# Joining two pairs of attention blocks in a fused attention and gated feed-forward kernel, and moving batches 2 and 3 to other slots

## The chip, the cores and the metric

The kernel runs on one core of one Trainium2 chip, in one launch. The metric is the device time of that launch in microseconds, and the figure that counts is the median over several executions. A profiled execution of the same program is shown as well; its time is given beside the span that its trace covers.

## The reference

Two blocks follow each other. The first is a polysketch attention with 4 batches, 4 heads, 1088 positions and a head size of 32. The second is a feed-forward block with a sigmoid gate over the 4 x 1088 = 4352 tokens that the first one gives, with a model size of 128 and an inner size of 1536.

```python
def phi(x):                       # r = 8, so 64 features
    a = np.einsum('rd,bhsd->bhsr', S1, x)
    b = np.einsum('rd,bhsd->bhsr', S2, x)
    return np.einsum('bhsi,bhsj->bhsij', a, b).reshape(*x.shape[:-1], r * r)
q_p, k_p = phi(q), phi(k)
kv  = np.einsum('bhsf,bhsd->bhfd', k_p, v)
z   = np.sum(k_p, axis=2)
num = np.einsum('bhsf,bhfd->bhsd', q_p, kv)
den = np.einsum('bhsf,bhf->bhs', q_p, z)[..., None] + 1e-06
x   = (num / den).transpose(0, 2, 1, 3).reshape(B * S, H * D)
out = (1 / (1 + np.exp(-(x @ w_gate))) * (x @ w_val)) @ w_out
```

The weights and the two sketch matrices come in as 64-bit floats and are turned into 32-bit ones on the chip.

## The kernel before

**The feed-forward part is the stream.** The tokens are cut into chunks of 512 (the last one 256). For each chunk, a *wave* (`w1`, L525 to L603) computes 128 gate columns and 128 value columns for all its tokens: four matmuls `wave<-xT,w_sb`, each on 64 of the 128 columns of TensorE's array, so that two run side by side. ScalarE takes the sigmoid of the gate (`sg`, L548), and VectorE multiplies (`g`, L583). There are 12 waves to a chunk (6 for the last), 102 in all, and a wave is called here by its number from 0, and so is the *slot* that ends with it. `slot` (L610) issues for each wave: the multiplication of the wave before, up to one late step of the result's sums, the output products that have come due, and then the wave. The output products of two waves (`w2_a`, `w2_b`, L460 and L490) are seven matmuls of 64 columns of weights against 256 tokens, four in one slot and three in the next; seven take the place of eight, for which GpSimd forms differences of `g` (`tsum`, L367) and VectorE sums of the results (`res`, L479). The waves have two PSUM buffers in the pool `psm`, tag `wave`.

**The attention is fed into the stream** in blocks between the waves, one batch after the other. For batch b:

- `load_kq(b)` and `load_v(b)` bring k, q and v into SBUF on SP's queue, `turn_k` and `turn_q` (two pieces, 512 and 576 wide) transpose them on VectorE.
- `begin(b)` (L1232) computes, on TensorE, the sketches of k (`kps`, 8 matmuls of 64 rows x 32 columns) and of q (`qcomp`: `cqps`, 8 matmuls likewise). ScalarE copies the second to SBUF (`cq`), and from there it is written to DRAM (`dq`). `spread(b)` (L834) reads it back in repeated form into `qp` and `bq`, and into the small tiles `A8` and `B8`: 14 loads on SP's queue, each of which also waits until the eighth load before it has landed.
- `outer(b, 0)` and `outer(b, 1)` multiply k's sketches into features (`KP`), `sum_z` adds them up, `qmult(b, 0)` and `qmult(b, 1)` multiply `qp` by `bq`.
- `kv(b)` (L888) is 36 matmuls of 128 rows x 32 columns against 64 features and 4 more for z; `kvd` copies the result out on ScalarE; `ndt` (L939) turns it with two matmuls of 128 x 64; `weights_z` (L993) prepares z on VectorE.
- `parts(b)` (L1266) is the last group: `den_j` (8 matmuls of 64 x 32 and a product on VectorE, `pd`), the numerators (`nps` in a wave buffer, `nps2`), `den_i` (2 matmuls), a copy of the numerators on ScalarE (`num`), and on VectorE the division, `turn_den` and then the products into `xT`, which the waves read.

All of kps, kv, ndt, denj and nps2 share one PSUM buffer (pool `ps2`, tag `two`). The tile `kq` of pool `ld` holds in turn k and q of a batch and its `bq`. `num` shares the buffer of `KP`.

**The order is written by hand.** Each of TensorE, VectorE, ScalarE and GpSimd executes its instructions in the order of the program text; SP's queue is ordered by the framework. For batches 2 and 3 the loop at L1344 takes the slot of each step from the table `plan` (L1342): `until(n)` issues slots until wave n is next. For batch 2: turn_k 27, turn_q 29 and 30, begin 31, outer 32 and 34, sum_z 36 and 37, kv 38, ndt 39, qmult 39 and 42, parts 44; for batch 3: 48, 49 and 51, 53, 56 and 57, 58 and 59, 60, 61, 61 and 63, 68. Batch 1 has begin at 13, kv at 18, ndt at 19, parts at 22.

```python
slot(lambda: ndt(1), 1)
slot(None, 1)
qmult(1, 1)
load_kq(2)
slot(None, 1)
slot(lambda: parts(1), 1)
```

Of the kernel before, what the change touches and what calls it, by code (L numbers as in the profile page):

```python
# [16 lines left out]
P = 128  # L17
# [3 lines left out]
def kernel(  # L21
# [31 lines left out]
    ld = ctx.enter_context(tc.tile_pool(name="ld", bufs=1))  # L53
    sbA = ctx.enter_context(tc.tile_pool(name="sbA", bufs=2))
    raw = ctx.enter_context(tc.tile_pool(name="raw", bufs=NJ // 2))
    sbN = ctx.enter_context(tc.tile_pool(name="sbN", bufs=1))
    sbG = ctx.enter_context(tc.tile_pool(name="sbG", bufs=3))

    dram = ctx.enter_context(tc.tile_pool(name="dram", bufs=1, space=bass.MemoryType.DRAM))

# [203 lines left out]
    k_t, q_t = {}, {}  # L264


    def new_kq(b):
        t = ld.tile([P, 2 * H * W1], F32, tag="kq", name="kq")
        kq = t[:, : 2 * T * D].rearrange("p (a t d) -> p a t d", a=2, t=T)
        k_t[b], q_t[b] = kq[:, 0], kq[:, 1]  # L270

# [20 lines left out]
    def warm(*cols):  # L292
        t = psm.tile([P, 2, 512], F32, tag="wave", name="warm")
        x = nc.const_aps.tensor(1.0, [P, P], F32)
        for n in cols:
            r = nc.const_aps.tensor(1.0, [P, n], F32)
            nc.tensor.matmul(out=t[:, 0, :n], lhsT=x, rhs=r, start=True, stop=True)  # L297
# [362 lines left out]
    WD = 160  # L660
    mask = {}

    def kps(b):
        t = ps2.tile([P, 2, 512], F32, tag="two", name="kps")
        ts = [t[:, 0], t[:, 1]]
        turns = [(g, pi) for g in range(4) for pi in range(2)]

        if b == 0:
            ts[1] = pso.tile([P, TCH], F32, tag="acc1", name="kps1")
            turns.sort(key=lambda x: x[1])  # L670
        for g, pi in turns:
            rows = slice(64 * pi, 64 * pi + 64)
            nc.tensor.matmul(  # L673
                out=ts[pi][32 * g : 32 * g + 32, : NJK * 32],
                lhsT=sk[rows, :],
                rhs=kT_of[b][rows, KBASE[g] : KBASE[g] + NJK],
                start=True,
                stop=True,
            )

        KAB[b] = sbA.tile([P, 2, NJK, 32], F32, tag="kab", name="kab")
        for pi in range(2):
            nc.vector.transpose(
                out=KAB[b][:, pi].rearrange("p j c -> p (j c)"), in_=ts[pi][:, : NJK * 32]
            )
        KP[b] = sbA.tile([P, 2, NJK, 2, F], F32, tag="kp", name="kp", bufs=1)
# [147 lines left out]
    def spread(b, ns, cq, put, get):  # L834
        p0 = 64 * ns[0]
        d = dram.tile([P, 2, W1], F32, tag="dq", name="dq")
        put.dma_start(out=d[p0:], in_=cq[p0:])
        for n in ns:
            for i, t in enumerate((QP[b], BQ[b])):

                for c in (0, 1) if i else (0,):
                    d0 = d[64 * n + 32 * c + 2 * i, 0]
                    rows = [[0, R], [8 * W1, R]] if i else [[8 * W1, 2 * R], [0, R]]
                    get.dma_start(  # L844
                        out=t[64 * c : 64 * c + 64 if i else P, n * H * W1 : (n + 1) * H * W1],
                        in_=bass.AP(
                            tensor=d0.tensor, offset=d0.offset, ap=rows + [[1, H * W1]]
                        ),
                    )
        if len(ns) < 2:  # L850
            return
        put = get

        B8[b] = sbA.tile([P, W1], F32, tag="b8", name="b8", bufs=1)
        A8[b] = sbA.tile([P, 2, WD], F32, tag="a8", name="a8", bufs=1)
        for x in range(2):
            for m in range(2):
                p0 = 64 * x + 32 * m
                for i, t in enumerate((A8[b], B8[b])):
                    d0 = d[2 * i + m, 0]  # L860
                    if i == 0:
                        offset, run = d0.offset + (W1 - WD) * x, [[W1, 2], [1, WD]]
                    else:
                        offset, run = d0.offset + W1 * x, [[1, W1]]
                    put.dma_start(
                        out=t[p0 : p0 + 32],
                        in_=bass.AP(tensor=d0.tensor, offset=offset, ap=[[8 * W1, 32]] + run),
                    )
# [16 lines left out]
                    skip_group_check=True,  # L885
                )

    def kv(b, zsum):  # L888
        kvz = KVZ[b] = ps2.tile([P, 2, 512], F32, tag="two", name="kvz")[:, 0]
        for j in [1, 2, 3, 4, 5, 6, 7, 8, 0]:  # L890
            for h in range(H):
                nc.tensor.matmul(  # L892
                    out=kvz[32 * h : 32 * h + 32, :F],
                    lhsT=v_sb[:, h, j, :],
                    rhs=KP[b][:, h // 2, j, h % 2, :],
                    start=(j == 1),
                    stop=(j == 0),
                    skip_group_check=True,
                )
        for h in range(H):  # L900
            nc.tensor.matmul(
                out=kvz[32 * h : 32 * h + 32, F : 2 * F],
                lhsT=nc.const_aps.tensor(1.0, [P, 32], F32),
                rhs=zsum[:, h, :],
                start=False,
                stop=True,
                skip_group_check=True,
            )
# [242 lines left out]
        start=True,  # L1151
        stop=True,
    )
    warm(64)
    st_ = st_[:, : 2 * R].rearrange("p (n r) -> p n r", n=2)
    sk = const.tile([P, 2, 2, R], F32, tag="sk")
    nc.vector.tensor_tensor(
# [71 lines left out]
    slot(None, 1)  # L1229
    cq = {}  # L1230

    def begin(b):  # L1232
        glu()
        kps(b)
        cq[b] = qcomp(b, (0, 1), (psm, "wave"))
        spread(b, (0, 1), cq[b], nc.scalar, nc.sync)

# [25 lines left out]
                    stop=True,  # L1263
                )

    def parts(b):  # L1266
        den_j(b)
        glu()
        t = psm.tile([P, 2, 512], F32, tag="wave", name="nps")
        numerators(b, t, False)  # L1270
        num = sbA.tile([P, 2, NJK, 2, F], F32, tag="kp", name="num", bufs=1)
        num = num.rearrange("p c j m f -> p (c j m f)")[:, :1024].rearrange("p (c w) -> p c w", c=2)
        nc.scalar.copy(out=num, in_=t)
        t = ps2.tile([P, 2, 512], F32, tag="two", name="nps2")
        numerators(b, t[:, :, WD : WD + 32], True)
        turn_den(b, den_i(b, t[:, 0, :WD]))
        for n in range(2):
            rb = sbA.tile([P, 9, 2, 32], F32, tag="rb", name="rb")
            t0, tn = q_chk[n]
            r0 = RC[b][:, n]  # L1280
            nc.vector.transpose(
                out=rb[:, :tn].rearrange("p t c s -> p (t c s)"),
                in_=bass.AP(
                    tensor=r0.tensor,
                    offset=r0.offset,
                    ap=[list(r0.ap[0]), [1, 2 * tn], [0, 32]],
                ),
            )
            for u0, u1, x in ((0, 8, num[:, :, 256 * n : 256 * n + 256]), (8, tn, t[:, :, WD : WD + 32])):
                if u0 < u1:  # L1290
                    o = b * S + 64 * (t0 + u0)
                    nc.vector.tensor_tensor(
                        out=xT[:, o : o + 64 * (u1 - u0)].rearrange("p (t c s) -> p c t s", c=2, s=32),
                        in0=x.rearrange("p c (t s) -> p c t s", s=32),
                        in1=rb[:, u0:u1].rearrange("p t c s -> p c t s"),
                        op=MUL,
                    )
        moe["ready"] = b * S + S
# [10 lines left out]
    load_kq(1)  # L1309
    slot(None, 1)  # L1310
    slot(lambda: part01(lambda: narrow_w(NJ - 1, 3)), 1)
    slot(last01, 1)
    load_v(1)
    turn_k(1)
    slot(None, 1)
    turn_q(1, 0)
# [12 lines left out]
    qmult(1, 0)  # L1329
    weights_z(1)  # L1330
    slot(lambda: ndt(1), 1)
    slot(None, 1)
    qmult(1, 1)
    load_kq(2)
    slot(None, 1)
    slot(lambda: parts(1), 1)
    moe["store"]()
# [1 line left out]
    def until(n):  # L1339
        slot(None, n - moe["n"])  # L1340

    plan = {2: (27, 29, 30, 31, 32, 34, 36, 37, 38, 39, 42, 44)}  # L1342
    plan[3] = (48, 49, 51, 53, 56, 57, 58, 59, 60, 61, 63, 68)
    for b in range(2, B):  # L1344
        at = iter(plan[b])
        until(next(at))
        turn_k(b)
        for n in range(2):
            until(next(at))
            turn_q(b, n)  # L1350
        until(next(at))
        slot(lambda: begin(b), 1)
        for pi in range(2):
            until(next(at))
            outer(b, pi)
        for step in range(2):
            until(next(at))
            sum_z(b, step)
        until(next(at))
        slot(lambda: kv_all(b), 1)  # L1360
        if b + 1 < B:
            load_v(b + 1)
        until(next(at))
        qmult(b, 0)
        slot(lambda: ndt(b), 1)
        weights_z(b)
        until(next(at))
        qmult(b, 1)
        load_kq(b + 1)
        until(next(at))  # L1370
        slot(lambda: parts(b), 1)
    slot(None, 10**3)


# [28 lines left out]
```

## Time and profile before

| | |
|---|---|
| median of 3 executions | 292.4 us (292.35 to 292.85) |
| profiled execution, its own time | 296.02 us |
| span of its trace | 294.1 us |
| TensorE clock granted, mean | 0.999 |
| TensorE busy | 288.8 us, 98% of the span |
| VectorE busy | 186.5 us, 63% |
| GpSimd busy | 160.6 us, 55% |
| ScalarE busy | 93.7 us, 32% |
| DMA | 24.23 MB, 82 GB/s over the span |

The trace lists each instruction with its engine (PE for TensorE's matmuls, PEld for its weight loads, DVE for VectorE, ACT for ScalarE, POOL for GpSimd, SPq and ACTq for the loads that these two issue), the line of the code, the tiles that it writes and reads, its form and how many were merged into a row. Times are microseconds from the first instruction; a bracket says how long the engine stood idle before, and what ended that. A matmul in 32-bit floats makes two records. The ends of matmuls are modelled and include their way through the array, so the start of one to the start of the next tells more than the length of a record.

### The profile page before, as it was taken

What the parts mean: (1) busy time and instruction counts of PE and PEld (TensorE: products, weight loads), DVE (VectorE), ACT (ScalarE), POOL (GpSimd) and SP (SyncE); (2) the same over time, 40 slices, a digit from 0 to 9 for tenths busy, and PEclk for the clock granted to TensorE, in tenths of its full rate; (3) what the DMA queues carried; (4) which work ended last, traced back from release to release, by engine and by line L of the source; (5) the groups of instructions that cost most, each with busy time, mean ns of one, the idle gap of its engine ahead of it and who ended that gap; (6) DMA issues with size and microseconds to landing.
All of it is one profiled execution on the core that took longest, in us unless ns stands there. A gap on an engine that the chain in (4) does not pass through costs nothing.

```text
span 294.1 us, 5762 instructions
## 1 busy us (share of the span) xinstructions
PE 288.8 (98%) x2264; PEld 156.6 (53%) x2264; DVE 186.5 (63%) x316; ACT 93.7 (32%) x172; POOL 160.6 (55%) x222
## 2 busy tenths in 40 slices
PE   8989999999999999999999999999999999999995
PEld 3543433355455455545555555554555555555895
DVE  5778789885656766677556696667436423552482
ACT  3386542321324222323224222323223223322321
POOL 2266544796535657655456498555456565646300
PEclk9999999999999999999999999999999999999999
DMA  7993613295640168416000474202000200020003
GB/s 219 347 336 68 150 39 125 74 180 137 186 97 0 19 163 159 133 50 177 12 0 2 129 174 106 37 0 38 1 0 2 36 2 0 0 31 7 0 4 54
DMA packets 28890, 24.23 MB, mean 82 GB/s; under 512 B 18560, under 2 KB 24064, under 8 KB 28864
## 3 DMA queue, kind: packets, MB, share of 16 engines
q1 hardware_dynamic: 25808, 21.95, 30.1%
q10 hardware_dynamic: 3056, 1.92, 2.3%
q8 instruction: 18, 0.29, 0.4%
q14 instruction: 8, 0.07, 0.1%
HBM read 20.60 MB, written 3.26 MB: 81 GB/s over the span
## 4 chain that ended last, share of the span: by engine, by line
PE 89%; DMA 7%; SPq 1%; DVE 0%; issue 0%; ACT 0%; DVEq 0%
PE wave L540 55%; PE prod L377 20%; DMA bq<-dq 5%; PE moeout L421 4%; PE moeout L447 2%; PE warm L297 1%; PE kps L673 1%; SPq L844 1%; PE nps L1258 1%; DMA s_in<-in_S_dram 1%; PE kvz L892 1%; PE cqps L819 1%; DMA dq<-cq 1%; DMA b<-dq 1%; PE denj L1021 0%; PE dps L1063 0%
## 5 line engine op out<-in xcount | busy, mean ns | idle before, releaser
L540 PE MATMUL wave<-xT,w_sb 128*64 128x512 f32 (+3 forms) x820 | 210.6, 566 | 0.0
L540 PEld LDWEIGHTS wave<-xT,w_sb 128*64 128x64 f32 (+1 forms) x820 | 85.4, 140 | 63.2 <-issue 51.0
L548 ACT ACTIVATE sg<-wave 128x512 f32<-128x512 f32 x102 | 60.9, 597 | 171.1 <-PE wave L540 163.2
L583 DVE TENSOR_TENSOR g<-wave,sg 128x512 f32<-128x512 f32 x96 | 65.9, 686 | 76.3 <-ACT sg L548 75.0
L367 POOL TENSOR_TENSOR tsum<-g 128x256 f32<-128x256 f32 x84 | 67.9, 810 | 29.7 <-DVE g L583 29.6
L367 POOL TENSOR_TENSOR tsum<-g,tsum 128x256 f32<-128x256 f32 x42 | 34.2, 814 | 57.8 <-DVE g L583 57.6
L377 PE MATMUL prod<-tsum,ws 128*64 128x256 f32 x252 | 62.8, 381 | 0.0
L377 PEld LDWEIGHTS prod<-tsum,ws 128*64 128x64 f32 x252 | 31.2, 137 | 16.0 <-issue 11.8
L377 PE MATMUL prod<-g,w_sb 128*64 128x256 f32 x168 | 34.7, 381 | 0.0
L367 POOL TENSOR_TENSOR tsum<-tsum,g 128x256 f32<-128x256 f32 x42 | 32.7, 779 | 3.3
L377 PE MATMUL prod<-tsum,w_sb 128*64 128x256 f32 x84 | 25.3, 383 | 0.0
L377 PEld LDWEIGHTS prod<-g,w_sb 128*64 128x64 f32 x168 | 16.0, 136 | 17.5 <-issue 14.7
L377 PE MATMUL prod<-g,ws 128*64 128x256 f32 x84 | 25.0, 379 | 0.0
L117 POOL TENSOR_TENSOR head<-head,tail 128x384 int32<-128x384 int32 (+1 forms) x10 | 9.9, 987 | 13.9 <-DVE head L111 12.6
L377 PEld LDWEIGHTS prod<-g,ws 128*64 128x64 f32 x84 | 11.5, 137 | 3.7
L421 PE MATMUL moeout<-g,w_sb 128*128 128x512 f32 (+1 forms) x28 | 12.5, 603 | 0.0
L377 PEld LDWEIGHTS prod<-tsum,w_sb 128*64 128x64 f32 x84 | 10.8, 137 | 3.0 <-issue 2.2
L872 DVE TENSOR_TENSOR qp<-qp,bq 128x1152 f32<-128x1152 f32 (+1 forms) x7 | 9.4, 1344 | 4.6 <-DMA a<-dq 4.6
L752 DVE TENSOR_TENSOR kp<-kab 128x1152 f32<-128x1152 f32 (+2 forms) x10 | 10.9, 1101 | 0.0
L576 DVE TENSOR_TENSOR g<-wave,sg 128x512 f32<-128x512 f32 x6 | 6.7, 1121 | 4.6 <-ACT sg L548 4.6
L479 DVE TENSOR_TENSOR res<-prod,other 64x512 f32<-64x512 f32 (+1 forms) x14 | 7.6, 544 | 3.1 <-DMA a<-dq 1.6
L514 DVE STREAM_TRANSPOSE o_sb<-res 64x512 f32<-64x512 f32 x14 | 9.6, 688 | 0.0
(129 smaller groups left out, 209.6 us busy)
## 6 DMA issues: line engine op xcount, KB each, us to landing
qp<-dq SPq DMA_DIRECT2D x7, 576.0 KB
bq<-dq SPq DMA_DIRECT2D x14, 288.0 KB
kq<-in_k_dram SPq DMA_DIRECT2D x3, 544.0 KB
kq<-in_q_dram SPq DMA_DIRECT2D x3, 544.0 KB
w_in<-in_moe_w_out_dram SPq DMA_DIRECT2D x6, 256.0 KB
w_in<-in_moe_w_gate_dram SPq DMA_DIRECT2D x5, 256.0 KB
w_in<-in_moe_w_val_dram SPq DMA_DIRECT2D x5, 256.0 KB
v<-in_v_dram SPq DMA_DIRECT2D x8, 144.0 KB
```

The costliest lines, as they stand in the source:

```text
L117: nc.gpsimd.tensor_tensor(out=head, in0=head, in1=tail, op=ALU.add)
L367: nc.gpsimd.tensor_tensor(out=t[:, u], in0=in0, in1=in1, op=ALU.subtract)
L377: nc.tensor.matmul(out=out, lhsT=lhsT, rhs=rhs, start=start, stop=stop, skip_group_check=True)
L421: nc.tensor.matmul(out=moe["acc"][d], lhsT=w_sb[:, 2, j, d], rhs=g[:, jj], start=(j == 0), stop=(j == NJ - 1),)
L479: nc.vector.tensor_tensor(out=out, in0=in0, in1=in1, op=op)
L514: nc.vector.transpose(out=o_sb[:64, d].rearrange("p t x -> p (t x)"), in_=r[:, 1 + 2 * d : 3 + 2 * d].rearrange("p u x -> p (u x)"),)
L540: nc.tensor.matmul(out=wv[d, which, jj * tw + o : jj * tw + o + tp], lhsT=w_sb[:, which, j0 + jj, d], rhs=xT[:, t0 + o : t0 + o + tp], sta ...
L548: nc.scalar.activation(out=sg, in_=wv[:, 0], func=ACTF.Sigmoid)
L576: nc.vector.tensor_tensor(out=g.rearrange("p (j u s y) -> p j y u s", j=2, u=2, y=4), in0=wv[:, 1].rearrange("p (j y u s) -> p j y u s", j ...
L583: nc.vector.tensor_tensor(out=g, in0=wv[:, 1], in1=sg, op=MUL)
L752: eng.tensor_tensor(out=KP[b][:, pi, j0:j1].rearrange("p j m (i l) -> p (j m) i l", i=R), in0=bass.AP(tensor=a0.tensor, offset=a0.offset, ...
L872: nc.vector.tensor_tensor(out=q0, in0=q0, in1=half(BQ[b], n), op=MUL)
```

## The change

**Two joined places.** `kps` takes an argument `also`: the kv of another batch is then written into free columns of the same PSUM tile, ahead of kps's own matmuls. `begin(3, 2)` uses it, so that kv(2) and the projections of batch 3 are one block at slot 35. `parts` takes the same argument: `parts(2, 3)` at slot 45 puts kv(3) between the second numerators and `den_i`, in free columns of their tile, and the copy of `num` behind it.

**Other slots.** The loop and its table are gone; the steps are written one by one. Batch 2: turn_k 20, turn_q 21 and 23, begin 24, outer 25 and 26, sum_z 28 and 30, kv 35, weights_z 36, ndt 37, qmult 38 and 44, parts 45. Batch 3: turn_k 32, turn_q 33, begin 35, outer 36 and 37, sum_z 40 and 42, kv 45, ndt 48, qmult 50 and 52, parts 56. On VectorE turn_k(2) now stands between g(18) and g(19), turn_q(2, 0) between qmult(1, 1) and g(20), and turn_q(2, 1) between the division of parts(1) and g(22).

**Loads and memory.** `load_kq(2)` stands behind `load_v(1)`, ahead of spread(1) on SP's queue; `load_kq(3)` at slot 23. k and q of batches 2 and 3 get a tile of their own (`kq2`) in a new pool `late`, which takes the space that the conversion of the weights (`sbN`) used, and so do A8 and B8 of batch 3. bq(3) shares its tile with bq(2) and waits for qmult(2, 1).

**At the start** a matmul that only keeps TensorE busy, `warm`, has 128 columns in place of 64.

```diff
+    late_pool = []
+
     def new_kq(b):
-        t = ld.tile([P, 2 * H * W1], F32, tag="kq", name="kq")
+        pool, tag, w = (ld, "kq", 2 * H * W1) if b < 2 else (late_pool[0], "kq2", 2 * T * D)
+        t = pool.tile([P, w], F32, tag=tag, name="kq")
...
-    def kps(b):
+    def kps(b, also=None):
         t = ps2.tile([P, 2, 512], F32, tag="two", name="kps")
+        if also is not None:
+            kv(also, ZS[also], t[:, 0, NJK * 32 : NJK * 32 + 2 * F])
...
-        B8[b] = sbA.tile([P, W1], F32, tag="b8", name="b8", bufs=1)
-        A8[b] = sbA.tile([P, 2, WD], F32, tag="a8", name="a8", bufs=1)
+        pool = late_pool[0] if b == B - 1 else sbA
+        B8[b] = pool.tile([P, W1], F32, tag="b8", name="b8", bufs=1)
+        A8[b] = pool.tile([P, 2, WD], F32, tag="a8", name="a8", bufs=1)
...
-    warm(64)
+    warm(128)
...
-    def begin(b):
+    def begin(b, also=None):
         glu()
-        kps(b)
+        kps(b, also)
+        if also is not None:
+            kvd(also)
...
-    def parts(b):
+    def parts(b, also=None):
...
-        nc.scalar.copy(out=num, in_=t)
+        first = t
         t = ps2.tile([P, 2, 512], F32, tag="two", name="nps2")
         numerators(b, t[:, :, WD : WD + 32], True)
+        if also is not None:
+            kv(also, ZS[also], t[:, 1, 4 * F : 6 * F])
+        nc.scalar.copy(out=num, in_=first)
         turn_den(b, den_i(b, t[:, 0, :WD]))
+        if also is not None:
+            kvd(also)
...
     slot(lambda: part01(lambda: narrow_w(NJ - 1, 3)), 1)
+    top.close()
+    late_pool.append(ctx.enter_context(tc.tile_pool(name="late", bufs=1)))
     slot(last01, 1)
     load_v(1)
+    load_kq(2)
     turn_k(1)
...
     slot(lambda: ndt(1), 1)
+    turn_k(2)
     slot(None, 1)
     qmult(1, 1)
-    load_kq(2)
+    turn_q(2, 0)
     slot(None, 1)
     slot(lambda: parts(1), 1)
...
+    until(23)
+    turn_q(2, 1)
+    load_kq(3)
+    until(24)
+    slot(lambda: begin(2), 1)
+    features(2, 25, 26, 28, 30)
+    until(32)
+    turn_k(3)
+    until(33)
+    turn_q(3, 0)
+    turn_q(3, 1)
+    until(35)
+    slot(lambda: begin(3, 2), 1)
+    load_v(3)
+    until(36)
+    weights_z(2)
+    outer(3, 0)
+    until(37)
+    outer(3, 1)
+    slot(lambda: ndt(2), 1)
+    qmult(2, 0)
+    until(40)
+    sum_z(3, 0)
+    until(42)
+    sum_z(3, 1)
+    until(44)
+    qmult(2, 1)
+    until(45)
+    slot(lambda: parts(2, 3), 1)
+    until(48)
+    weights_z(3)
+    slot(lambda: ndt(3), 1)
+    until(50)
+    qmult(3, 0)
+    until(52)
+    qmult(3, 1)
+    until(56)
+    slot(lambda: parts(3), 1)
```

More of the change, by code (lines that the diff above doesn't have):

```diff
@@ L55 @@
     raw = ctx.enter_context(tc.tile_pool(name="raw", bufs=NJ // 2))
-    sbN = ctx.enter_context(tc.tile_pool(name="sbN", bufs=1))
     sbG = ctx.enter_context(tc.tile_pool(name="sbG", bufs=3))
+    top = ExitStack()
+    sbN = top.enter_context(tc.tile_pool(name="sbN", bufs=1))
     dram = ctx.enter_context(tc.tile_pool(name="dram", bufs=1, space=bass.MemoryType.DRAM))
@@ L886, in kv0, with kv @@
                 )
-    def kv(b, zsum):
-        kvz = KVZ[b] = ps2.tile([P, 2, 512], F32, tag="two", name="kvz")[:, 0]
+    def kv(b, zsum, kvz=None):
+        if kvz is None:
+            kvz = ps2.tile([P, 2, 512], F32, tag="two", name="kvz")[:, 0]
+        KVZ[b] = kvz
         for j in [1, 2, 3, 4, 5, 6, 7, 8, 0]:
@@ L1340, in until, with features @@
         slot(None, n - moe["n"])
[L1342 to L1371, printed above, removed]
+    def features(b, *at):
+        steps = [(outer, 0), (outer, 1), (sum_z, 0), (sum_z, 1)]
+        for n, (step, i) in zip(at, steps):
+            until(n)
+            step(b, i)
+    until(23)
[36 more added lines that the diff above has]
+    slot(lambda: parts(3), 1)
     slot(None, 10**3)
```

## The prediction

> **What bounds the kernel now.** I read the page first: engine shares, then the chain that ended last.
>
> ```profile
> PE 288.8 (98%) x2264; PEld 156.6 (53%) x2264; DVE 186.5 (63%) x316; ACT 93.7 (32%) x172; POOL 160.6 (55%) x222
> ...
> PE 89%; DMA 7%; SPq 1%; DVE 0%; issue 0%; ACT 0%; DVEq 0%
> ```
>
> TensorE is the bound; the other engines matter only where they make it wait. So three things can move the time: TensorE's own work, what it loses at each change of tile shape, and its few waits. In the chain in order of time, an undisturbed stretch gives the price of work:
>
> ```profile
> 230.92 1.72 PE wave L540 x8
> ...
> 240.81 1.72 PE wave L540 x8
> ```
>
> Four waves with their products take 240.81 - 230.92 = 9.89 us, 2.47 a slot. A wave is 8 records of 512 columns on two column halves side by side in 1.72 us: 0.43 us for a record of 512 columns. By that price a kv block (40 matmuls of two records, 64 columns, four at a time) needs 20 x 64 columns, 1.07 us; kps and cqps 0.48 each; a parts block (denj 0.27, nps 0.86, nps2 0.05, den_i 0.27) 1.45. The timeline of TensorE around kv(2) shows what it really costs:
>
> ```profile
> 118.05 1.94 PE L540 MATMUL wave<-xT,w_sb 128*64 128x512 f32 x8
> 119.92 1.21 PE L892 MATMUL kvz<-kp,v 128*32 128x64 f32 x72
> 120.95 0.29 PE L901 MATMUL kvz<-zs,const-float32-1.0 128*32 128x64 f32 x8
> 121.17 0.65 PE L377 MATMUL prod<-g,w_sb 128*64 128x256 f32 x4
> ```
>
> The wave's last column enters at 118.05 + 1.72 = 119.77, the products resume at 121.17: 1.40 us for 1.07 of work, 0.33 lost on the way in and out. In the same way begin(2) (101.30 to 102.52) loses 0.25 and parts(2) (136.53 to 138.38) 0.40. ndt, which keeps the stream's shape, takes its own 0.22 and loses nothing.
>
> The one large wait is at parts(1). TensorE's timeline there, then VectorE's:
>
> ```profile
> 75.89 0.48 PE L1021 MATMUL denj<-b,zw 64*32 64x160 f32 x8
> 76.79 0.48 PE L1021 MATMUL denj<-b,zw 64*32 64x160 f32 x8 [0.42 <-DMA b<-dq]
> 77.06 1.16 PE L1258 MATMUL nps<-qp,nd 64*32 64x512 f32 x32
> 78.15 0.49 PE L1034 MATMUL nps<-pd,head 128*64 128x160 f32 x4
> ```
>
> ```profile
> 75.05 1.36 DVE L872 TENSOR_TENSOR qp<-qp,bq 128x1152 f32<-128x1152 f32 x1 [2.62 <-DMA a<-dq]
> 76.32 0.68 DVE L583 TENSOR_TENSOR g<-wave,sg 128x512 f32<-128x512 f32 x1
> 77.32 0.49 DVE L1029 TENSOR_TENSOR pd<-denj,a 128x320 f32<-128x320 f32 x1 [0.31 <-PE denj L1021]
> 77.73 0.68 DVE L583 TENSOR_TENSOR g<-wave,sg 128x512 f32<-128x512 f32 x1
> ```
>
> TensorE is there at 75.86 and resumes the products at 78.47: 2.6 us for 1.45 of work, about 0.8 more than parts(2) loses. Two things end this wait together. The last b8 piece lets denj finish (76.79 + 0.27 = 77.06). And nps takes the wave buffer of slot 20, which g(20) frees at 76.32 + 0.68 = 77.00; g(20) stands behind qmult(1,1), which stood for its data until 75.05.
>
> [...] 0.25 to 0.40 lost at the blocks of another shape, none at ndt. [...] an instruction queued ahead of g(20) delays it whole; g(20) at 76.32, long after its sigmoid (73.71 + 0.60), is that case. [...] Here the warm-up records of 512 columns start 0.85 us apart until 13.3 us, twice the 0.43 of later.
>
> **The change part by part.**
>
> *Join 1* (kv(2) inside begin(3), at slot 35). Matmuls and columns are the same; one way in and one way out are gone (of kv's 0.33), one change from 128x32 to 64x32 tiles is new. The trace shows no such change at full clock. Bounds: 0 if it costs all that is saved, -0.33 if nothing. I take -0.2. kvd(2) (0.37) now stands before cq (0.64) on ScalarE; the next sigmoid waits for kps, cqps, products and half a wave (2.5 us) anyway: nothing.
>
> *Join 2* (kv(3) inside parts(2), at slot 45). Likewise: kv's way in and out goes, a change to 128x32 between nps2 and den_i comes. Again -0.2 (0 to -0.33). The copy of num moves behind kv(3), because its tile has KP(3)'s buffer. It starts at kv's end and takes 1.01 us; VectorE wants it about 1.9 us after den_i (dTi to rb, 138.60 to 140.63 in parts(2)), and the wave buffer it empties is wanted only by slot 46. With kvd(3) it is 1.4 us on ScalarE, while the next sigmoid's gate comes 0.27 + 0.65 + 0.86 us after kv: nothing. Without that cover it would be 1 us.
>
> *Where the blocks fall.* A w2_b gives two of its three products to one column half, so after an odd number of them one half is 0.43 us behind, and a block that drains both halves there loses it. The sigmoids show the state: with no block near they follow at 2.6, 2.19, 2.6, 2.51, while at 93.72, 96.32, 98.92 and 101.52 the steps are 2.5, 2.6, 2.6, 2.6, without the short one: there such a loss is paid. Counted by slot, before has four of these half-losses: kv(1) at 18, the first w2_b of the next chunk at 29, begin(2) at 31, and 41. After has four: kv(1), begin(2) at 24, join 1 at 35, 41. Nothing; a miscount is worth 0.43 either way.
>
> *turn_q(2,0) to slot 21*, right behind qmult(1,1) and ahead of g(20), pd and g(21). It costs 0.69 us (mean of 128x512), 0.62 start to start. qmult(1,1) still waits for its DMA until 75.05, so g(20) ends at 77.00 + 0.62 = 77.62, and nps, which I find bound by g(20) and denj within 0.06 us of each other, starts at 77.68 in place of 77.06. pd, g(21) and all behind follow. Bounds: 0 if nps has no need of g(20), 0.69 at most. I take +0.62. This is the largest term.
>
> *turn_k(2)* (1.30) between g(18) and g(19): g(19) at 72.2 in place of 71.74, needed by wave 21 at 73.92: hidden.
>
> *turn_q(2,1)* (0.76) behind the division of parts(1), ahead of g(22). g(22) ended at 83.49; it now ends at 84.2 on the same scale. cqps of begin(2) wants its buffer: wave 23 ends at 83.63, plus 0.09 and kps's 0.51: 84.23. With the semaphore +0.05; 0 to +0.72.
>
> *Other VectorE work.* The fullest slot of after lies between g(28) and g(29): two res (0.41 + 0.98) and three sums (0.80 + 0.84 + 0.83), 3.9 us where 1.9 are free, so g(29) is 1.9 late. Wave 31 wants it 0.86 + 0.86 + 1.72 + 0.65 = 4.1 us after its gate, of which sigmoid and product take 1.3: 2.8 to spare. Hidden, as is the same sum between g(40) and g(41).
>
> *Loads on SP.* kq(2) (2 x 544 KB) stands before spread(1), in space freed by the last conversion of weights (45.63 + 0.93 = 46.6). kq(1), as large, was issued at 42.14 and turned from 48.71; the trace has no DMA at all from 48 to 54, and spread(1)'s write starts at 54.60. So kq(2) is there in time. Behind it stand spread(1), v(2) (75.4, as before) and kq(3), now at about 84 for use at slot 32: 20 us spare. The four bq(3) loads wait for qmult(2,1) at slot 44, and stand behind six stores that are ready one slot earlier; spread(2) took 17 us from 105.55 for twice the bytes, and qmult(3,0) comes 6 slots and join 2, 18 us, later. Nothing; without the spare each us late is a us. *A8/B8 of batch 3* in own buffers: only removes a wait.
>
> *warm(128)*: two records of 64 more columns at half clock, about 0.1 us each way, in front of kps at 6.30, whose sk is ready at 6.11. +0.1; if it made the clock come earlier, the cold kps, aps and bps (3.3 us) would shrink: down to -0.8, an estimate from half of that with VectorE and ScalarE between. I take +0.1.
>
> Sum: -0.2 - 0.2 + 0.62 + 0.05 + 0.1 = +0.37 us on the profiled execution's 296.02 (span 294.1 and 1.9 around it): 296.4. The median of the runs shown is 3.6 lower; the same difference gives 292.8.
>
> **The rivals.**
>
> *B, the turn is hidden:* nps is bound by the b8 DMA alone, or qmult's data come a little earlier. For: denj's wait names that DMA, and the two times coincide. Against: the buffers of the waves are two, and g(20) ended 0.06 us before nps. Then -0.2 - 0.2 + 0.1: 292.1.
>
> *C, slower: the second turn isn't covered.* Place: turn_q(2,1) ahead of g(22), just before begin(2). The cover is 84.23 - 83.49 = 0.74 us for 0.72. If kps comes sooner, or VectorE's division later than 82.9, each 0.1 us costs 0.1, to 0.72 in all; from some 0.25 us on it decides. Then +0.37 + 0.67: 293.4. For: the cover is a coincidence. Against: everything before it shifts alike.
>
> *D, faster:* the start gets its full clock earlier: 292.8 - 0.9 = 291.9, or less where join savings reach their ends: 291.6. [...]
>
> *E, the loads collide:* kq(2) is issued late and shares the queue with spread(1). 1.1 MB took 4.4 us for kq(1); all of it at parts(1): 297. Against: the gap from 48 to 54.
>
> **How the numbers follow.** No change is what a measurement can't tell from 292.4: 0.2%, 0.58 us, so 291.8 to 293.0. A (292.8) has 0.56, B 0.18, C 0.16, D 0.08, E 0.02. A alone lies in 292.4 to 293.2: three quarters in the band, the rest above. B is in the band but for 0.02, C and E above it, D below. Same 0.42 + 0.16 = 0.58; slower 0.14 + 0.18 = 0.32; faster 0.02 + 0.08 = 0.10. The range for 8 in 10 takes in B's low end (292.4 - 0.56 with both joins at their ends, 291.9) and C: 291.9 to 293.5.
>
> **What would show it.** Joins: TensorE from the wave's end to the first product, 2.4 us at join 1 (1.07 + 0.97 + 0.35) and 3.0 at join 2; if 2.65 and 3.25, they save nothing. The turn: at parts(1) nps 0.6 us after denj's end, with g(20) behind the qT row. B: nps right behind denj. C: a gap between kps and cqps at begin(2). D: dps well before 13.27. The forecast is wrong if TensorE waits on a place not named here, above all at slots 24 to 31, where VectorE is fullest.

## The result, and the profile after

The kernel after takes 293.97 us (median of 7 runs, 293.12 to 294.36), the kernel before 292.77 (7 runs beside them, 292.35 to 293.07): ratio 1.0041, 95% interval 1.0027 to 1.0055. It is 1.2 us slower, where 0.4 was forecast, and outside the range of 291.9 to 293.5. One caution for all that follows: the profiled execution of before (296.02) was no usual one. Its first sigmoid of the stream began at 19.40 us, in every other profile taken here, of either kernel, at 16.76 to 17.35, and TensorE kept the slow rate of the start for longer: its 16 records of kps took 1.21 us there (at 6.30), 0.72 in the changed kernel's profile (at 6.01). So stretches are compared from there on.

The page after, engine shares and the chain that ended last:

```profile
PE 285.7 (98%) x2264; PEld 156.8 (54%) x2264; DVE 185.0 (63%) x316; ACT 93.7 (32%) x172; POOL 164.4 (56%) x222
...
PE 86%; DMA 7%; DVE 3%; issue 1%; ACT 1%; SPq 1%; POOL 0%; DVEq 0%
```

TensorE is still the bound, but its share of the chain fell from 89 to 86%, and VectorE is in it with 3%. The price of the undisturbed stream is unchanged; the chain in order of time has four waves with their products in 241.42 - 231.53 = 9.89 us:

```profile
231.53 1.72 PE wave L544 x8
...
241.42 1.72 PE wave L544 x8
```

So the loss lies at places, and there are three. The first is parts(1); TensorE's timeline, then VectorE's, then GpSimd's:

```profile
73.20 0.72 PE L1030 MATMUL denj<-b,zw 64*32 64x160 f32 x16
74.38 1.15 PE L1269 MATMUL nps<-qp,nd 64*32 64x512 f32 x32 [0.46 <-DVE g L587]
75.46 0.49 PE L1043 MATMUL nps<-pd,head 128*64 128x160 f32 x4
```

```profile
71.60 1.53 DVE L879 TENSOR_TENSOR qp<-qp,bq 128x1152 f32<-128x1152 f32 x1 [1.37 <-DMA b<-dq]
73.05 0.70 DVE L657 STREAM_TRANSPOSE qT<-kq 128x512 f32<-128x512 f32 x1
73.68 0.65 DVE L587 TENSOR_TENSOR g<-wave,sg 128x512 f32<-128x512 f32 x1
...
76.39 0.72 DVE L1058 TENSOR_SCALAR rci<-dTi 128x20 f32<-128x20 f32 x2
```

```profile
75.46 0.73 POOL L371 TENSOR_TENSOR tsum<-g,tsum 128x256 f32<-128x256 f32 x1 [0.33 <-DVE g L587]
76.27 0.73 POOL L371 TENSOR_TENSOR tsum<-tsum,g 128x256 f32<-128x256 f32 x1
```

nps now waits for g(20) alone, which ends at 74.33 behind turn_q(2,0); TensorE's rows don't name the b8 data any more. The bracket says 0.46 us, but from sigmoid 21 to sigmoid 22 the wait costs 5.28 - 4.39 = 0.89 (4.39 is this step in the seven profiles without a wait, below). For comparison, TensorE's rows in d_both44, one of those seven:

```profile
73.53 0.50 PE L1030 MATMUL denj<-b,zw 64*32 64x160 f32 x16
73.83 1.16 PE L1269 MATMUL nps<-qp,nd 64*32 64x512 f32 x32
```

There nps begins 0.30 us after denj, while denj's records still run; in the changed kernel 1.18 after it. The difference is the whole 0.89, within rounding: from the start of nps to sigmoid 22 both take 4.21. The bracket counts only from the modelled end of denj's records, so it understates the wait.

Further down on VectorE, rci begins just after the start of a sum on GpSimd (76.27) and ends just after its end (77.00): its two rows take 0.72 us. In d_both44 its first row meets only the last part of a sum, which ends at 76.10, and the two take 0.38; GpSimd's row, then VectorE's:

```profile
75.37 0.73 POOL L371 TENSOR_TENSOR tsum<-g,tsum 128x256 f32<-128x256 f32 x1 [0.90 <-DVE g L587]
75.84 0.38 DVE L1058 TENSOR_SCALAR rci<-dTi 128x20 f32<-128x20 f32 x2
```

The second place is begin(2), on TensorE:

```profile
81.04 0.72 PE L679 MATMUL kps<-kT,sk 64*32 64x288 f32 x16
81.93 0.72 PE L825 MATMUL cqps<-qT,skq 64*32 64x288 f32 x16 [0.17 <-DVE g L587]
```

cqps comes 0.89 us after kps (0.5 where it doesn't wait) and waits for g(22). Sigmoid 22 to 25 takes 9.42 us here, 9.02 in the best profiles: 0.40. Measured from sigmoid 22, rci begins at the same point in every profile (2.19 to 2.20 before it). With turn_q(2,1) ahead of g(22) and a short rci, as in d_join44, g(22) begins 2.30 us after the sigmoid and cqps 3.01; here 2.64 and 3.35. So 0.35 of the 0.40 is the longer rci, and 0.05 the turn.

The third is behind join 2. TensorE's timeline, then its weight loads:

```profile
138.11 0.50 PE L1030 MATMUL denj<-b,zw 64*32 64x160 f32 x16
138.40 1.16 PE L1269 MATMUL nps<-qp,nd 64*32 64x512 f32 x32
139.55 1.21 PE L901 MATMUL nps<-kp,v 128*32 128x64 f32 x72
140.55 0.32 PE L910 MATMUL nps<-zs,const-float32-1.0 128*32 128x64 f32 x8
140.81 0.49 PE L1043 MATMUL nps<-pd,head 128*64 128x160 f32 x4
141.13 0.38 PE L381 MATMUL prod<-tsum,ws 128*64 128x256 f32 x1
...
143.29 0.65 PE L544 MATMUL wave<-xT,w_sb 128*64 128x512 f32 x2 [0.27 <-issue]
```

```profile
141.57 0.57 PEld L544 LDWEIGHTS wave<-xT,w_sb 128*64 128x64 f32 x4
143.29 0.14 PEld L544 LDWEIGHTS wave<-xT,w_sb 128*64 128x64 f32 x2 [1.15 <-issue]
```

The join itself is as long as forecast (138.11 to 141.13). Then, in the middle of a wave, with no semaphore named and none in the program at that instruction, the weight loads stop for 1.15 us, and the matmuls stand idle for 0.27. Sigmoid 44 to 45 takes 6.23 us. The list of DMA queues for 140.9 to 143 us has one piece of 16 KB on a queue for instructions:

```profile
q8 instruction: 1, 0.02, 2.9%
```

In the record of the single packets it runs from 141.00 to 141.96. None lies between 118.0 and it. That this queue brings TensorE's instructions is read from its number of pieces: 18 in the whole run, one for some 250 of TensorE's loads and matmuls.

Join 1 is undisturbed:

```profile
110.33 1.21 PE L901 MATMUL kps<-kp,v 128*32 128x64 f32 x72
111.36 0.29 PE L910 MATMUL kps<-zs,const-float32-1.0 128*32 128x64 f32 x8
111.59 0.72 PE L679 MATMUL kps<-kT,sk 64*32 64x288 f32 x16
112.10 0.69 PE L825 MATMUL cqps<-qT,skq 64*32 64x288 f32 x16
112.72 0.43 PE L381 MATMUL prod<-tsum,w_sb 128*64 128x256 f32 x1
```

From 110.33 to 112.72 are 2.39 us, 2.4 was forecast.

### The profile page after: what moved, and what is told of

It is laid out like the page before. It is cut to its first block, busy times and chain, and to the rows that moved or that the text cites. A ratio compares the mean times of both kernels' runs of the same rounds, so it can differ in the third digit from the quotient of the medians.

```text
span 292.2 us, 5763 instructions
## 1 busy us (share of the span) xinstructions
PE 285.7 (98%) x2264; PEld 156.8 (54%) x2264; DVE 185.0 (63%) x316; ACT 93.7 (32%) x172; POOL 164.4 (56%) x222
## 4 chain that ended last, share of the span: by engine, by line
PE 86%; DMA 7%; DVE 3%; issue 1%; ACT 1%; SPq 1%; POOL 0%; DVEq 0%
PE wave L544 54%; PE prod L381 19%; DMA qp<-dq 4%; PE moeout L425 4%; PE moeout L451 2%; DMA b<-dq 2%; PE nps L1269 1%; DMA s_in<-in_S_dram 1%; PE cqps L825 1%; DMA dq<-cq 1%; PE kps L679 1%; SPq L850 1%; DVE rb L1297 0%; PE nps L1091 0%; PE nps L1043 0%
## 5 line engine op out<-in xcount | busy, mean ns | idle before, releaser
L371 POOL TENSOR_TENSOR tsum<-g 128x256 f32<-128x256 f32 x84 | 72.8, 869 | 26.1 <-DVE g L587 25.9
L371 POOL TENSOR_TENSOR tsum<-g,tsum 128x256 f32<-128x256 f32 x42 | 32.8, 780 | 58.5 <-DVE g L587 58.1
L381 PE MATMUL prod<-tsum,ws 128*64 128x256 f32 x252 | 62.0, 381 | 0.0
```

The lines of the kernel that those rows point to most:

```text
L371: nc.gpsimd.tensor_tensor(out=t[:, u], in0=in0, in1=in1, op=ALU.subtract)
L381: nc.tensor.matmul(out=out, lhsT=lhsT, rhs=rhs, start=start, stop=stop, skip_group_check=True)
```

## The experiments

Four groups, each on another chip and timed beside runs of the kernel before, so medians of different groups are best compared by their ratio to before. "Stream" is the time from sigmoid 12 to sigmoid 99 of the profile, 230.12 in a second profile of before, 230.98 after.

**First group: before once more, the stop, the turns, the warm-up.**

*b_again*, the kernel before, unchanged.

> The kernel before, unchanged, for a second profile: that of its shown profile began with a clock that came late (first sigmoid of the stream at 19.40 us, against 16.81 in the changed kernel's profile). If that was one execution's accident, the first sigmoid lies near 16.8 us and the span some 2.6 us lower, about 291.5; then the start has nothing to do with the difference of the medians. If the late clock belongs to the kernel, the sigmoid stays at 19.4. At parts(1) this profile also tells what the wait there is worth when the stream starts earlier: 0.42 us before denj as shown, or less.

Its first sigmoid begins at 17.16, its own time is 293.46: the late start was one execution's. At parts(1) it waits for the b8 data (0.25 us before denj), and the step there is 5.14 us, so this execution loses 0.75 in its turn. Of 59 runs of the kernel before in this group 35 are below 292.9 us, down to 292.19, the others go up to 293.77. A loss of 0.75 hardly fits into the lower ones, so more than half of them probably have no such wait; no profile shows one of these.

*a_split8:*

```diff
+half = tp // 2 if 13 <= moe["n"] < 21 else tp
+for e in range(o, o + tp, half):
     nc.tensor.matmul(
-        out=wv[d, which, jj * tw + o : jj * tw + o + tp], ...
+        out=wv[d, which, jj * tw + e : jj * tw + e + half], ...
```

> The changed kernel; in the waves of slots 13 to 20 each matmul of 512 columns is two of 256. TensorE's columns stay the same, its instruction stream gets 128 longer ahead of join 2. Theory F (TensorE runs out of instructions in join 2: a 16 KB piece of the instruction queue[...] starts at 141.0 us, 2.3 us after the join's first half, while 280 instructions are used up in 3 us; the wave after it stops in its middle from 142.1 to 143.3): the pieces fall elsewhere, the stop goes, and the time drops 0.6 us, ratio to the changed kernel 0.998. Rival (the stop comes from the join itself, its change of tile shape, the late copy of num or the copy of kv(3)): no change, the stop stays after join 2.

293.16 us, ratio to before 1.0021 (1.0011 to 1.0032), 0.8 below the changed kernel. The stop is gone. TensorE's timeline behind join 2:

```profile
140.42 0.49 PE L1045 MATMUL nps<-pd,head 128*64 128x160 f32 x4
...
141.60 1.88 PE L546 MATMUL wave<-xT,w_sb 128*64 128x512 f32 x7
```

Seven records run on without a break, and sigmoid 44 to 45 takes 5.74: 0.49 gained. The 128 more instructions weren't free: against d_both44 below they cost 0.35 us over the eight slots and about as much again where they end (2.58 in place of 2.19 from sigmoid 20 to 21). But with TensorE that much later, the waits of parts(1) and begin(2) are gone in this profile, 0.89 and 0.35. By place: 0.49 + 0.89 + 0.35 - 0.7 = 1.03, and the stream is 1.01 shorter (229.97).

*a_turns:*

```diff
     turn_k(2)
     slot(None, 1)
-    qmult(1, 1)
     turn_q(2, 0)
+    turn_q(2, 1)
+    qmult(1, 1)
...
     until(23)
-    turn_q(2, 1)
```

> The changed kernel with turn_q(2,0) and turn_q(2,1) both ahead of qmult(1,1), into the 1.37 us in which VectorE waits for the b8 data there. Theory T (the two turns stand ahead of g(20) and g(22), which nps of parts(1) and cqps of begin(2) wait for): the gap of 0.46 us at nps shrinks to 0.1 or less, the one of 0.17 before cqps goes with the 0.2 to 0.4 that the two halves of the array lose around it; together -0.8 us, to about 293.2. Rival (nps is then held by the b8 data as it is in the kernel before, and begin(2) loses the same by its place after an odd number of w2_b's): -0.1 to -0.4.

292.94 us, ratio 1.0005 (0.9996 to 1.0014): 1.0 below the changed kernel. The profile is of the slowest of its 22 executions (293.89). There the b8 data came late and held denj twice (0.42 and 0.41), and four stores on ScalarE's queue took 3.54 us to issue (2.01 in the changed kernel's), ahead of sigmoid 23. For that reason sigmoid 22 to 25 takes 9.38 here, though kps and cqps follow each other without a gap and rci is short; in the profile of d_j36_44 below it is the same (3.49 us of stores, 9.34). So what the edit gives is in the median; this trace shows what still varies. It shows something on the stop, too. Four profiles have the stop, and in all four it falls at the same instruction, after 287 loads and matmuls from the join's begin. In each the loads go on 1.2 to 1.3 us after the end of the instruction piece, and the stop is the longer, the later the piece comes after the join's begin:

```
               join begins  piece           loads go on  gap of loads
changed          138.11     141.00-141.96     143.29        1.29
a_warm64         138.94     141.84-142.80     144.11        1.28
d_turn0          138.14     140.51-141.88     143.11        1.09
a_turns          138.52     140.76-141.91     143.21        0.80
```

(The gap counts from the start of the last load.) In a_turns the piece begins 2.24 us after the join's begin (2.89 in the changed kernel's); a gap of 0.80 us in the loads costs nothing there: sigmoid 44 to 45 takes 5.73 (5.74 in a_split8, without a stop).

*a_warm64:* `warm(128)` back to `warm(64)`.

> The changed kernel with the warm-up of 64 columns as it was before. If the 128 columns only cost their own time: -0.1 us. If they change when the clock is released: the stream's first sigmoid moves from 16.8 us by more than 0.3 either way, and the time with it. If nothing: within 0.1.

293.94 us, ratio 1.0031 (1.0018 to 1.0044), not to be told from the changed kernel's 1.0041; an effect of 0.1 us wouldn't show in this spread. The first sigmoid is at 17.35, in other profiles with 128 columns at 16.76 to 17.31. Six of its 22 executions lie at 292.32 to 292.93. So a kernel with the changed order doesn't lose its 1.2 us every time, only in most executions.

**Second group: both mends, and each join undone.**

*c_best:* the edits of a_split8 and a_turns together.

> The changed kernel with both edits: the two turns ahead of qmult(1,1), and the waves of slots 13 to 20 in halves of 256 columns. If the two losses are separate (the turns' at parts(1) and begin(2), and the stop behind join 2), they add: 293.97 - 1.0 - 0.5 (the stop alone, by the step at slot 45; the other 0.3 that the halves brought lay at begin(2), which the turns now mend) = 292.4, ratio to before 0.999. If the turns' run had lost the stop already in most of its executions, nothing is left to add: 292.9, ratio 1.0005.

292.86 us, ratio 1.0010 (1.0002 to 1.0018): they don't add. No wait is left at parts(1), at begin(2) or behind join 2, but the halved waves keep their price. The seven profiles without a wait at parts(1) (a_split8, this one and the three below, d_join44, d_both44) have the step of 4.39 or 4.40 us.

*c_nojoin1* (on c_best):

```diff
-    slot(lambda: begin(3, 2), 1)
+    slot(lambda: begin(3), 1)
+    slot(lambda: kv_all(2), 1)
```

> The kernel with both edits, and join 1 undone: begin(3) alone at slot 35, kv(2) as a block of its own at slot 36. Theory J (a join saves one way in and out, 0.23 by the lengths of the blocks, and the count of half-losses stays at four): +0.2 against the kernel with both edits. Rival (the join saves nothing, the change from 128x32 to 64x32 tiles inside it costs as much): 0. By place: from the wave's end to the products, begin(3) 1.2 and kv(2) 1.4, 2.6 together, where the join has 2.4.

293.14 us, 0.28 above c_best; stream 230.12 against 229.93, 0.19 more. The join saves what was forecast.

*c_nojoin2* (on c_best):

```diff
+    slot(lambda: kv_all(3), 1)
-    slot(lambda: parts(2, 3), 1)
+    slot(lambda: parts(2), 1)
```

> The kernel with both edits, and join 2 undone: kv(3) as a block of its own at slot 44, parts(2) alone at slot 45, the copy of num at once behind its products. Theory J: +0.2. Rival (the join saves nothing, or its late copy of num and the dense run of small matmuls cost what it saves): 0 or less than the joined kernel, to -0.3.

293.04 us, 0.18 above c_best, but the stream only 0.08 longer (230.01). Between the two: this join saves 0.1 to 0.2. The intervals of the two ratios overlap (1.0015, 1.0008 to 1.0021, against 1.0010, 1.0002 to 1.0018), but no loss from the late copy of num shows.

*c_turn0* (on c_best): turn_q(2,1) back ahead of g(22).

> The kernel with both edits, but only turn_q(2,0) ahead of qmult(1,1): turn_q(2,1) stands again ahead of g(22). If the wait for g(22) at begin(2) is the larger part (0.4 of the 0.9 read from the two profiles at parts(1) and begin(2)): +0.4 against the kernel with both edits, with a gap before cqps. If parts(1) was all: 0. If the extra matmuls of the halves give VectorE the time it lacked, as the trace with them alone had no gap at begin(2): 0 to +0.1.

292.92 us; from sigmoid 22 to 25 9.07 us, 0.06 more than c_best. With the cover intact the second turn costs just the 0.05 of the forecast, so the 0.40 in the changed kernel isn't its own. ("Cover" is the time by which g(22) ends before cqps wants its buffer.)

**Third group: the stop by other means, one turn alone, sums.**

*d_join44:*

```diff
-    until(44)
+    until(43)
     qmult(2, 1)
-    until(45)
+    until(44)
     slot(lambda: parts(2, 3), 1)
```

> The changed kernel with join 2 one slot earlier, at 44 (qmult(2,1) at 43), nothing else. Theory F (the stop behind join 2 comes from where the pieces of TensorE's instructions fall: one begins some 30 instructions into the join at slot 45, and the join and the slot behind it use it up before the next has come): a slot earlier the piece begins some 60 instructions into it, the join is over before it is used up, no stop, -0.5 us. Rival (the stop belongs to the join, its tile shapes or its copies): the stop moves along with it, 0.

293.32 us (292.09 to 294.17), ratio 1.0006 (0.9989 to 1.0023). The stop is gone though the join, its tiles and its copies are all there; TensorE's timeline after it:

```profile
137.55 0.49 PE L1043 MATMUL nps<-pd,head 128*64 128x160 f32 x4
...
138.73 1.89 PE L544 MATMUL wave<-xT,w_sb 128*64 128x512 f32 x8
```

Sigmoid 43 to 46 is 0.45 us shorter than in the changed kernel. This execution began 0.5 us late, its b8 data were there in time, and neither parts(1) nor begin(2) waits; 10 of its 14 executions lie above 292.9.

*d_turn0:* turn_q(2,0) alone ahead of qmult(1,1).

> The changed kernel with turn_q(2,0) alone ahead of qmult(1,1); turn_q(2,1) stays ahead of g(22). Theory P (one cause for both waits: turn_q(2,0) makes g(20) and with it g(21) late; GpSimd's sums of g(21) then begin just ahead of VectorE's first rci row of parts(1), which lasts to the end of the sum, 0.65 us in place of 0.30; so g(22) is late for cqps): both go, -0.5 to -0.9. Rival (turn_q(2,1) itself makes g(22) late): the gap at nps goes, the one before cqps stays, and -0.1 to -0.4 is left.

292.87 us, ratio 1.0008 (0.9995 to 1.0020): about 1.0 below the changed kernel, at the upper end of theory P or beyond. The profile is of an execution of 293.88 us, where both waits are still there, for the data came late again: qmult(1,1) from 72.00, g(20) to 74.33, nps at 74.39, GpSimd's sum at 76.30 to 77.03 and rci from 76.39 to 77.06. Here g(20) is late with no turn in front of it, and rci and g(22) are late all the same: that bears out the order of causes. In all fourteen profiles of the first three groups, the two of before and the one of after among them, the first rci row of parts(1) ends 0.03 to 0.04 us after the end of a sum on GpSimd. It lasts 0.64 to 0.67 in the three where nps waits for g(20) alone, and 0.20 to 0.30 in the others. Behind join 2 in the changed kernel (141.73) no sum runs beside this row, and it lasts 0.18.

*d_both44:* a_turns and d_join44 together. *d_j36_44:* the same with join 1 at slot 36.

> The changed kernel with both turns ahead of qmult(1,1) and join 2 at slot 44, without the halved waves that cost TensorE 0.35 us in the kernels that had them: the sum of the mends without their price. 293.97 - 0.5 (stop) - 0.9 (waits at parts(1) and begin(2)) = 292.5, ratio to before 0.999. If the b8 data then hold denj at parts(1), as in the profile with the turns alone (0.42 and 0.41), up to 0.8 of it comes back: 292.9 or more.

292.88 us (292.17 to 293.78), ratio 1.0000 (0.9987 to 1.0014). The profile shows no wait anywhere past the start, and a stream of 229.24 us. The second profile of before has 230.12, or 229.37 without the 0.75 at parts(1).

> As the kernel with both turns and join 2 at slot 44, and join 1 at slot 36 in place of 35 (outer(3,1) and ndt(2) one slot later). By the count of half-losses (0.43 us where a block falls while one column half is behind) the joins at 35 and the first w2_b of the chunk at 41 cost one each; with the join at 36 neither does, but each of the two is followed by other parity: the count of this stretch falls from two to none, and one half-record of 0.43 is gained in the end: -0.4 against the kernel with join 1 at 35. If there are no such losses: 0.

292.48 us (292.14 to 293.83), ratio 0.9997 (0.9981 to 1.0013), not to be told from the one with the join at 35. By place: from sigmoid 34 to 43 it is 0.1 shorter, not 0.43; its profile has the late b8 data at parts(1) (293.83). The count of half-losses isn't borne out here.

**Fourth group: what decides parts(1).**

*e_bturn*, the kernel before with

```diff
     qmult(1, 1)
+    extra = const.tile([P, P], F32, tag="extra", name="extra")
+    for j in range(4):
+        nc.vector.transpose(out=extra, in_=w_sb[:, 0, j, :])
```

> The kernel before with four transpositions of 128 columns (about 0.8 us on VectorE, of weights, into a tile that nobody reads) between qmult(1,1) and g(20), where the change has turn_q(2,0). Theory G (this place, g(20) behind whatever VectorE does after the b8 data have come, is what makes the changed kernel slow in nearly all of its executions, where the kernel before loses it only in those whose data are late): the median rises by 0.5 to 0.8, and the executions below 292.9, about half of those of the kernel before, are gone; nps waits for g(20). Rival (the data decide in both kernels, the turn adds nothing): within 0.2 of the kernel before.

293.84 us, ratio 1.0037 (1.0021 to 1.0053); two of ten executions below 292.9, against 19 of 32 of the kernel before beside it. The transpositions took 1.34 us rather than 0.8. VectorE's timeline, then TensorE's:

```profile
71.95 1.84 DVE L872 TENSOR_TENSOR qp<-qp,bq 128x1152 f32<-128x1152 f32 x1 [1.74 <-DMA b<-dq]
73.71 1.34 DVE L1336 STREAM_TRANSPOSE extra<-w_sb 128x128 f32<-128x128 f32 x4
74.97 0.65 DVE L583 TENSOR_TENSOR g<-wave,sg 128x512 f32<-128x512 f32 x1
```

```profile
75.68 0.66 PE L1258 MATMUL nps<-qp,nd 64*32 64x512 f32 x8 [1.49 <-DVE g L583]
```

Work of VectorE at this place and nothing else of the change makes the kernel before as slow as the changed one. The place is shown with this, the turn's own price is not: the work was twice as long as the turn (0.70).

*e_bb8:* the kernel before, qmult(1,1) behind g(20), the four b8 loads of a batch ahead of its a8 loads. *e_ab8:* the same two edits on d_j36_44.

> The kernel before with qmult(1,1) issued behind g(20), and the four b8 pieces of each batch loaded ahead of the four a8 pieces. If its slower executions are those in which nps and denj of parts(1) wait for these data (0.75 to 1.0 us in the two profiles): they become rare, the median falls by 0.3 to 0.6, to about 292.3, ratio 0.998 to 0.999. If they come from the start or elsewhere: no change.

292.76 us (but for one run 292.58 to 293.13), ratio 1.0000 (0.9978 to 1.0023): both ends of the spread are gone, the median isn't lower. At parts(1) the step is 4.70 us: nps now waits for qmult(1,1) in place of g(20) and begins 0.3 later than without a wait, a small price for a large one in some executions.

> The changed kernel with every mend: the two turns ahead of slot 21, join 1 at slot 36, join 2 at slot 44, qmult(1,1) behind g(20), b8 ahead of a8. Stream without waits 0.1 to 0.3 shorter than that of the kernel before without its waits: 292.0 to 292.2, ratio 0.9975, and 0.1 to 0.3 below the kernel before with the same two edits. If the joins' 0.28 are eaten by something else: level with that one.

292.70 us (292.39 to 293.00), ratio 1.0002 (0.9994 to 1.0010), level with e_bb8 within 0.1, though its stream is 0.19 shorter (229.48 against 229.67). No version made here beats the kernel before by more than a measurement tells.

## Why the prediction was wrong, step by step

Two terms of the sum failed. Behind join 2 it had nothing, and a stop of TensorE there cost some 0.47 us; at begin(2) it had +0.05, and 0.40 was lost there. Together they are 0.8 us, as much as the forecast of +0.4 falls short of the measured 1.2. The other terms held, or their errors are too small to tell.

- **The joins' saving: right.** 0.2 each was taken; 0.2 to 0.3 for join 1 and 0.1 to 0.2 for join 2 was measured by undoing them. Both blocks have the forecast lengths (2.39 and 3.02).
- **"Join 2 ... nothing" behind it: wrong, by 0.45 to 0.49 us.** The step asked for the tile shapes, the copy of num and ScalarE, and all three were harmless (d_join44 has them all and no stop). It didn't ask what TensorE's instructions need. Counted in the trace, some 270 loads and matmuls start in the 3.0 us of the join, where the undisturbed stream starts 12 in a us. The trace has 18 pieces of 16 KB on the instruction queue for 2264 loads and 2264 matmuls, and one of them lands at 141.96, 1.33 us before the loads go on. Shifting the instructions, or the join by a slot, takes the stop away; in four executions it falls at the same instruction, and its end follows the piece by 1.2 to 1.3 us. That the stop hangs on the piece is shown by this; what sets the time of the piece is not, nor whether the other transfers in flight at that time (the bq loads among them) delay it.
- **turn_q(2,0) "+0.62" at parts(1): the right place, mechanism and size, on a base that was no usual one.** nps does follow g(20), g(20) the turn, the turn qmult(1,1), and the turn takes 0.63 us of this row (73.05 to 73.68). The other 0.26 of the 0.89 is what the late data would have cost without it: an estimate, by taking 0.63 from the start of nps. But the term was added to a profile that already lost 0.99 us there (5.38 - 4.39), and more than half of the executions of the kernel before probably lose nothing. The changed kernel loses 0.89 here and, by the spread, something like it in most executions, the kernel before 0.75 to 1.0 in the minority. With half of those averaged out that is about +0.5, an estimate. In the two profiles themselves the difference is -0.1. Rival B is refuted by the rows above and by e_bturn.
- **turn_q(2,1) "+0.05": right in itself (c_turn0), wrong in place, 0.40 in all.** Rival C's mark, a gap between kps and cqps, is there, and so is a cost (0.40, where it had 0.67). But g(22) was late because "VectorE's division" was, as C allowed, and that through the late g(20). With it the distance between GpSimd's sums, which follow g(21), and rci changes, and rci meets the beginning of a sum in place of the end of one. Each first rci row that begins during a sum ends 0.03 to 0.04 us after that sum (fourteen profiles); what holds the row until then, no run shows. The working had GpSimd in no term.
- **warm(128) "+0.1" and rival D: neither shows** (a_warm64), and 0.1 is too small to be seen there.
- **The half-losses "net 0": not contradicted, and not shown.** The one test of the count found 0.1 where it says 0.43.
- **"The same difference gives 292.8": not a safe step.** The profiled execution stood 3.3 us above the median then measured, for a late start (2.2 us at the first sigmoid) and late data (0.99). The second profile of before, which starts 2.24 us sooner, loses 0.75 at parts(1) in place of 0.99: a difference found there needn't hold in the executions around the median. Nothing warned of it but the distance to the median.

The sum by place: parts(1) about +0.5, begin(2) +0.40, the stop +0.47, the joins -0.3: +1.07 of the 1.2 measured. About 0.15 stays without a place; between d_both44 and the second profile of before without its wait it is the same 0.15.

## What to carry to other kernels

Before adding an operation to an in-order queue, look at what stands there between late data and a buffer that the bounding engine wants; and do so in more than one execution, since the one at hand may have the slack used up or untouched. Packing small matmuls together saved part of the ways in and out (0.1 to 0.3 us a join here), but count their instructions against the interval of the instruction pieces (one for some 250 loads and matmuls here): the same block stopped the engine at slot 45 and not at slot 44. A small VectorE row on a critical chain can last until the GpSimd operation beside it ends, as rci did here (up to 0.67 us, 0.18 with no sum beside it).

## What the runs showed that was not expected

- TensorE stopped 0.80 to 1.29 us in its weight loads with no semaphore behind it, until 1.2 to 1.3 us after a 16 KB instruction piece had landed.
- A VectorE row of 128x20 lasted 0.20 to 0.67 us at parts(1), in fourteen profiles always to the end of a GpSimd sum, and 0.18 where no sum ran beside it.
- A wait of 0.46 us by its bracket cost 0.89 from sigmoid to sigmoid, one of 0.25 cost 0.75: the bracket begins at the modelled end of the record before, and without a wait nps begins well ahead of that end.
- Cutting matmuls of 512 columns into halves of 256 cost 0.05 us a wave, and 0.4 more where they ended ahead of parts(1).
- Executions of one and the same kernel spread over 1.1 to 2.5 us, single outliers apart. In the profiles the stream's first sigmoid (16.76 to 19.40 us), the time at which qmult(1,1) begins after its wait for DMA (54.79 us after that sigmoid in the changed kernel's, 55.65 in the first of before), and the time that four stores on ScalarE's queue take to issue (2.0 to 3.5 us) differ. Two kernels with slack at parts(1) spread over 0.3 to 0.6 (c_best, e_ab8).
